# Retention outputs in two visits of TensorE instead of three, and the last product of the kernel in two halves

## The chip, the cores and the metric

The kernel runs on one core of a Trainium2 chip. A core has a matrix engine (TensorE, PE in the profile, its weight loads PEld), a vector engine (VectorE, DVE), a scalar engine (ScalarE, ACT), GpSimd (POOL) and SyncE (SP), which here issues the transfers. Each takes its instructions in its own order and waits on semaphores for the others. Operands lie in SBUF, and TensorE writes to PSUM, which has eight banks of 2 KB for each of 128 partitions. The metric is the device time of one execution in microseconds (us).

## The reference

Two parts follow each other. The first is a retention layer over 4 sequences of 768 tokens with 8 heads of 64:

```python
for t in range(S):
    state = gamma * state + einsum('bhd,bhe->bhde', k[:, :, t], v[:, :, t])
    y[:, :, t] = scale * einsum('bhd,bhde->bhe', q[:, :, t], state)
```

Its output, as 3072 tokens of 512 features, goes through a two-layer block: `h = x @ w_in` (512 to 2048), `g = where(h > 0, h, exp(min(h, 0)) - 1)`, `out = g @ w_out` (2048 to 512). All is fp32.

## The kernel before

**Blocks.** The 3072 tokens are taken in six blocks of 512, each of four chunks of 128 tokens; the code counts blocks (`tb`) from 0, the text from one, so block six is `tb` 5. A sequence has six chunks, so that blocks two and five (`tb` 1 and 4) hold the end of one sequence and the start of the next, and there the powers of gamma start again in the middle of the block.

**Large products.** Nearly all of TensorE's time goes to the two layers. They use the seven-product scheme for 2x2 blocks of matrices, once or twice nested, with sums of inputs and outputs on VectorE (`quarters_of`, the L945 and L815 groups; L990 and L1407 for outputs) and copies of partial results on ScalarE (L986, L1297, L1403). Their results go to PSUM banks that the code calls pa (two buffers), pb and pd (one each). A fp32 product instruction appears as two records in the trace.

**Retention.** Time runs through it in half chunks of 64 tokens. A block takes three kinds of 64x64 products, each of which uses one quarter of the array: a half of its rows (`sub` or `a`) and a half of its columns (`c`).

- scores (L331): q against k in each half chunk, 128 records for a block; VectorE masks them (L342).
- states (L371): k against v in each half chunk, 128 or 112 records; VectorE adds the states up, one after the other (L383), the last of a block into `carry`.
- outputs: within a half chunk, v against the masked scores (`within`, L427, 128 records for a block), and across, the state against q (`across`, L442, 128 or, where a sequence starts, 112 records). Both add up in the same PSUM tile y. VectorE then multiplies y by powers of gamma into the input x of the first layer (L417, tiles xt or xb).

A product that takes array rows of half `a` must not write to a bank to which one of the other half still writes. Within products of half chunk `sub` use row half `sub`; across products of head half `a` use row half `a`. In the kernel before, a bank y[sub] belongs to one half chunk and holds all heads, so across products with `a` equal to `sub` can follow the within products at once, and the others (`other` = 1) need a wait. The wait goes through VectorE: it copies eight numbers a partition out of each bank (`seen`, L411), and the other products wait for that copy.

**The visits.** A block's outputs are made in halves of two chunks (`outputs(tb, pp)`), two banks each, from the pool `ps_r` of four buffers (tag "r"), which scores, states and outputs use in turn. `outputs_step` runs the generators. In blocks two to four (`tb` up to 3) step 0 does half 0 up to the copies; step 1 ends half 0 (other products, two multiplications) and begins half 1; step 2 ends half 1. In blocks five and six step 0 begins half 0, step 1 begins half 1, step 2 ends both. So TensorE leaves the large products for outputs three times a block.

The order on each engine is the order of the Python calls. The steps stand between large products by hand: in the loop over `inner` for block two, in the first `sec` loop for block three, in the loop over `ORDER1` for block four, and at the places `VISITS` of the last loop for blocks five and six.

**The end.** `inner_end` makes the last seven products. The last one (k = 3) adds into the bank pa that already holds three products; VectorE then adds the kept part `k[:, 0, 1]`, and a store of 128 KB ends the kernel (L1465 to L1467).

Of the kernel before, what the change touches and what calls it, by code (L numbers as in the profile page):

```python
# [28 lines left out]
def kernel(  # L29
# [281 lines left out]
    def state(tb, n):  # L311

        if n % (2 * CPB) == 0:
            return carry[(tb + n // (2 * CPB)) % 2]
        if (tb, n) == (0, 3):

            return xt[0].rearrange("p a t -> p (a t)")[:, 0:256].rearrange("p (h e) -> p h e", e=D)

        k = raw[tb * CPB + (n - 1) // 2][1][:, 1].rearrange("p h d -> p (h d)")
        return k[:, (n - 1) % 2 * 256 : ((n - 1) % 2 + 1) * 256].rearrange("p (h e) -> p h e", e=D)  # L320

    def fresh(tb, n):

        return (tb * 2 * CPB + n) % (S // D) == 0
# [122 lines left out]
    def outputs_of_first():  # L447

        y = [bank(x).rearrange("p a (b x d) -> p (a b) x d", b=2, x=2) for x in "bd"]
        for x in range(2):  # L450
# [19 lines left out]
            if not x:  # L470
                yield

    def outputs_step(tb, step):

        if step == 0:
            held["y"] = [outputs(tb, pp) for pp in range(2)]
        early_end = tb <= 3
        if step and early_end:
            next(held["y"][step - 1], None)
        elif step == 2:  # L480
            for g in held["y"]:
                next(g, None)
        if step < 2:
            next(held["y"][step])
            next(held["y"][step])

    half = [slice(0, TH), slice(TH, TB)]

# [368 lines left out]
    def done(name):  # L857
        slot, lasts = where.pop(name), lasting.pop(name)
        if lasts or wanted and wanted[0][0][0] == 1:
            slots.append((slot, lasts))  # L860
        fetch()
# [518 lines left out]
    def second_big(nb, behind_last):  # L1380
        ts, kept2 = {}, {}
        ends = nb == NB - 1

        def input_parts(j):
            x = INPUT2[j]
            t = (slots_e, slots_s)[len(ts) % 2]
            b11, b12, b21, b22 = (quarter(x, a, b) for a in range(2) for b in range(2))
            yield from quarters_of(t, b11, b12, b21, b22, nc.gpsimd if j == 1 else nc.vector)
            ts[j] = {1: b11, 2: b21, 3: b22, 4: t[3], 5: t[0], 6: t[1], 7: t[2]}

        def product(j, k, ps, begin):
            name = (nb + 2, j, k)
            w = where[name].rearrange("p (f d) -> p f d", f=4)
            for f in range(4):
                nc.tensor.matmul(  # L1395
                    ps, lhsT=w[:, f, :], rhs=ts[j][k][:, f // 2, f % 2, :], start=(begin and f == 0), stop=(f == 3),
                    skip_group_check=True,
                )
            done(name)

        def copy(ps):
            m = small.tile([P, TH], FP32, name="ms", tag="ms")
            nc.scalar.copy(m, ps)  # L1403
            return m

        def add(o, x, y):
            nc.vector.tensor_tensor(out=o, in0=x, in1=y, op=ALU.add)  # L1407

        part = lambda x: bank(x)[:, 0]

        def inner(j):
            res = (two if j in (6, 7) else mpool).tile([P, 2, 2, TH], FP32, name="res", tag="m")
            pa = part("a")
            product(j, 1, pa, True)
            m1 = copy(pa)
            pb = part("b")
            product(j, 2, pb, True)
            add(res[:, 0, 0], pb, m1)
            yield
            product(j, 6, pa, False)  # L1420
            u2 = copy(pa)
            pd = part("d")
            product(j, 7, pd, True)
            yield
            product(j, 5, pa, False)
            add(res[:, 1, 1], pd, copy(pa))
            yield
            product(j, 3, pa, False)
            nc.scalar.copy(res[:, 0, 1], pa)  # L1429
            yield  # L1430
            product(j, 4, pd, False)
            add(res[:, 1, 0], pd, u2)
            sum_up(j, res.rearrange("p d t c -> p (d t c)"))

        def inner_end(j):

            res = mpool.tile([P, 2, 2, TH], FP32, name="res", tag="m")
            to = out_of[nb][1, 0].rearrange("p (d t c) -> p d t c", d=2, t=2)
            k = kept2[6].rearrange("p (d t c) -> p d t c", d=2, t=2)
            pa = part("a")  # L1440
            product(j, 1, pa, True)
            m1 = copy(pa)
            pb = part("b")
            product(j, 2, pb, True)
            add(res[:, 0, 0], pb, m1)
            yield
            product(j, 6, pa, False)
            u2 = copy(pa)
            pd = part("d")
            product(j, 7, pd, True)  # L1450
            m7 = copy(pd)
            yield
            add(u2, u2, k[:, 1, 0])
            add(u2, pd, u2)
            product(j, 5, pa, False)
            add(res[:, 1, 1], pa, m7)
            yield
            add(res[:, 0, 0], res[:, 0, 0], k[:, 0, 0])
            nc.sync.dma_start(to[:, 0, 0], res[:, 0, 0])
            add(res[:, 1, 1], res[:, 1, 1], k[:, 1, 1])  # L1460
            pb = part("b")
            product(j, 4, pb, True)
            add(res[:, 1, 0], pb, u2)
            nc.sync.dma_start(to[:, 1], res[:, 1])
            product(j, 3, pa, False)  # L1465
            add(res[:, 0, 1], pa, k[:, 0, 1])
            nc.sync.dma_start(to[:, 0, 1], res[:, 0, 1])  # L1467

        def store(name, h):
            nc.sync.dma_start(out_of[nb][int(name[1]) - 1, int(name[2]) - 1], h)  # L1470

        def sum_up(j, m):

            kept2[j] = m
            if j == 2:
                add(m, kept2[1], m)
                store("C11", m)
            elif j == 6:
                add(m, kept2[1], m)
            elif j == 5:  # L1480
                add(m, kept2[6], m)
                add(kept2[6], kept2[6], kept2[7])
                add(kept2[7], m, kept2[7])
# [12 lines left out]
        for at, j in enumerate(BIG2):  # L1496
            cur = (inner_end if j == 4 and ends else inner)(j)
            next(cur)
            if j == 1:
                yield "tail"  # L1500
            for _ in before:
                pass
            if at:
                yield "first"
            some(changes, {2: 1, 3: 4, 7: 1, 5: 2}.get(j, 0))
            parts = input_parts(BIG2[at + 1]) if at + 1 < 7 else iter(())
            if j == 1:

                next(cur)
                yield "elu"  # L1510
                some(parts, 2)
            else:
                some(parts, 2)
                if at == 6:
                    behind_last()
                next(cur)
                yield "middle"
            next(cur)
            if j != 1:
# [179 lines left out]
    def retention_step(tb, step):  # L1699
        if step == 0:  # L1700
            scores(tb, 0)
            scores(tb, 1)
        elif step == 1:
            states(tb, 0)
            states(tb, 1)
        else:
            outputs_step(tb, step - 2)
# [123 lines left out]
    for nb in range(NB):  # L1831
# [83 lines left out]
        for at, (j, sub) in enumerate(ORDER1):  # L1915
# [18 lines left out]
            if nb == 0:  # L1934
                if at == 0:
                    scores(3, 1)
                elif at == 1:
                    retention_step(3, 3)
            if at == 7:
                run(tail)  # L1940
                seeds(0, 1, first=True)
# [2 lines left out]
            if nb == 0:  # L1944
                if at == 0:
                    states(3, 1)
                elif at == 1:
                    retention_step(3, 4)
                    run(tail)
            side(at, 2)  # L1950
# [81 lines left out]
        if more:  # L2032
# [1 line left out]
                scale_v(groups[0] * CPB + n)  # L2034
        step = 0
        VISITS = [
            (0, "end"), (1, "end"), (2, "middle"), (2, "end"), (3, "middle"),
            (5, "first"), (5, "end"), (6, "first"), (6, "middle"), (6, "end"),
        ]
        LOADS = [(3, "middle"), (3, "end"), (4, "first"), (4, "middle")]  # L2040
# [70 lines left out]
```

## Time and profile before

| what | value |
|---|---|
| median of 3 runs | 608.09 us (608.03 to 612.51) |
| the profiled execution's own time | 607.38 us |
| its span, first to last instruction | 605.6 us |
| TensorE busy | 599.0 us, 99% |
| VectorE busy | 508.6 us, 84% |
| ScalarE, GpSimd busy | 261.5 us and 98.3 us |
| granted TensorE clock | 1.000 |

The page gives busy times by engine, the chain of waits that ended last, and groups of equal instructions. A timeline row has start, length, engine, line, operation, output and inputs with shape, and the count of records merged; square brackets hold the idle time before it and what ended that. A merged row's length runs from its first start to its last end, and a record's end overlaps the next one's start. The chain of waits gives start, length and piece, with a product's length up to the next one's start.

### The profile page before, as it was taken

How to read it: one execution, taken by the hardware profiler on the slowest of the kernel's cores; microseconds unless marked ns; L12 is line 12 of the kernel's file. 1: busy time of each engine (PE TensorE's matmuls, PEld its weight loads, DVE VectorE, ACT ScalarE, POOL GpSimd, SP SyncE). 2: the span in 40 equal slices, each digit the busy share in tenths (PEclk: the TensorE clock that was granted, in tenths of full speed). 3: DMA queues.
4: the chain of work that ended last, by engine and by line, in shares of the span. 5: the costliest groups of instructions: out<-in, count | busy, mean ns of one | idle time of the engine just before them, and what ended most of it. 6: DMA issues, size and time to landing. Idle time of an engine off the chain costs nothing.

```text
span 605.6 us, 13752 instructions
## 1 busy us (share of the span) xinstructions
PE 599.0 (99%) x5510; PEld 491.9 (81%) x5510; DVE 508.6 (84%) x779; ACT 261.5 (43%) x448; POOL 98.3 (16%) x77
## 2 busy tenths in 40 slices
PE   7999999999999999999999999999999999999997
PEld 5865568888889999888766888888888866888886
DVE  6778889989899886899898887898658999779785
ACT  6898734205543112247589210100236779611110
POOL 2020000000230110000797000120000398000000
PEclk9999999999999999999999999999999999999999
DMA  8797578789968998698976445874555676556552
GB/s 324 274 407 289 189 232 254 227 244 268 351 224 264 354 348 294 204 307 272 352 248 217 129 131 153 273 277 112 197 167 151 172 221 194 160 150 188 154 152 115
DMA packets 85680, 139.85 MB, mean 231 GB/s; under 512 B 6896, under 2 KB 46576, under 8 KB 80880
## 3 DMA queue, kind: packets, MB, share of 16 engines
q1 hardware_dynamic: 85616, 138.96, 70.9%
q8 instruction: 44, 0.72, 0.5%
q14 instruction: 20, 0.16, 0.1%
HBM read 105.12 MB, written 33.82 MB: 229 GB/s over the span
## 4 chain that ended last, share of the span: by engine, by line
PE 97%; DMA 1%; DVE 1%; issue 0%; SPq 0%; ACT 0%
PE pa L1395 16%; PE pa L1286 9%; PE pd L1395 8%; PE pa L784 5%; PE pd L1286 5%; PE x L1349 4%; PE pb L1395 4%; PE pa L978 4%; PE pa L557 3%; PE x L647 3%; PE pb L1286 2%; PE pd L784 2%; PE pa L647 2%; PE pa L1336 2%; PE sc L331 2%; PE kv L371 2%
## 5 line engine op out<-in xcount | busy, mean ns | idle before, releaser
L1403 ACT COPY ms<-pa 128x256 f32<-128x256 f32 x41 | 15.3, 372 | 106.5 <-PE pa L1395 103.5
L1395 PE MATMUL pa<-gC,wq 128*128 128x256 f32 x240 | 56.8, 381 | 0.0
L1395 PEld LDWEIGHTS pa<-gC,wq 128*128 128x128 f32 x240 | 45.1, 190 | 7.3 <-issue 1.0
L305 POOL TENSOR_TENSOR chunk<-chunk,vf 128x512 f32<-128x512 f32 x15 | 19.6, 1316 | 153.6 <-DMA chunk<-in_qkv_dram 104.7
L1362 ACT ACTIVATE r<-r 128x512 f32<-128x512 f32 x64 | 40.4, 631 | 2.0
L1407 DVE TENSOR_TENSOR res<-pd,ms 128x256 f32<-128x256 f32 x26 | 11.0, 422 | 28.2 <-PE pd L1395 17.5
L1297 ACT COPY m<-pa 128x512 f32<-128x512 f32 x32 | 18.7, 584 | 35.0 <-PE pa L1286 31.8
L1395 PE MATMUL pd<-w_all,wq 128*128 128x256 f32 x120 | 28.3, 379 | 0.0
L1363 DVE SCALAR_TENSOR_TENSOR gC<-r,gC 128x512 f32<-128x512 f32 x24 | 27.9, 1169 | 0.0
L926 POOL TENSOR_TENSOR wp<-wp 128x512 fp32r<-128x512 f32 x6 | 8.8, 1467 | 116.5 <-DMA scratch_dram<-wi 102.2
L183 ACT ACTIVATE w_all<-wraw 128x1024 uint32<-128x1024 uint32 (+1 forms) x19 | 19.2, 1009 | 15.1 <-PE x L647 9.6
L1395 PEld LDWEIGHTS pd<-w_all,wq 128*128 128x128 f32 x120 | 22.8, 190 | 3.1
L1857 POOL TENSOR_TENSOR chunk<-chunk,w_all 128x512 f32<-128x512 f32 x4 | 5.1, 1287 | 124.4 <-ACT w_all L1297 124.4
L1377 DVE TENSOR_TENSOR gC<-w_all,gC 128x1024 f32<-128x1024 f32 x20 | 24.2, 1260 | 0.0
L1349 PE MATMUL x<-xl,wq 128*128 128x512 f32 x64 | 23.7, 457 | 0.0
L1395 PE MATMUL pa<-w_all,wq 128*128 128x256 f32 x96 | 22.9, 381 | 0.0
L1395 PE MATMUL pa<-ts,wq 128*128 128x256 f32 x96 | 22.9, 381 | 0.0
L185 ACT ACTIVATE w_all<-wraw 128x1024 fp8e4<-128x1024 f32 (+1 forms) x19 | 22.6, 1190 | 0.6
L1395 PE MATMUL pd<-ts,wq 128*128 128x256 f32 x96 | 22.7, 379 | 0.0
L557 PE MATMUL pa<-xb,w_all 128*128 128x512 f32 x48 | 21.5, 597 | 0.0
L1429 ACT COPY res<-pa 128x256 f32<-128x256 f32 x13 | 4.8, 373 | 38.1 <-PE pa L1395 38.1
L213 DVE CUSTOM_DVE_ANT_0 w_all<-wraw,w_all 128x2048 uint16<-128x2048 uint16 (+1 forms) x19 | 20.1, 1059 | 0.8
(369 smaller groups left out, 1598.6 us busy)
## 6 DMA issues: line engine op xcount, KB each, us to landing
wq<-scratch_dram SPq DMA_DIRECT2D x231, 256.0 KB, 3.4
chunk<-in_qkv_dram SPq DMA_DIRECT2D x22, 1024.0 KB, 7.5
wraw<-in_w_dram SPq DMA_DIRECT2D x15, 1024.0 KB, 5.9
scratch_dram<-wp SPq DMA_DIRECT2D x8, 512.0 KB, 3.9
out_dram<-res SPq DMA_DIRECT2D x7, 512.0 KB, 3.4
scratch_dram<-gT SPq DMA_DIRECT2D x12, 256.0 KB, 3.6
wq<-scratch_dram SPq DMA_DIRECT2D x24, 128.0 KB, 2.9
scratch_dram<-w_all SPq DMA_DIRECT2D x12, 256.0 KB, 3.1
```

The costliest lines, as they stand in the source:

```text
L185: nc.scalar.activation(top, hi.bitcast(FP32), AF.Copy, scale=2.0**-120, saturate=False)
L213: vec.tensor_tensor(out=flat, in0=c, in1=flat, op=ALU.add)
L557: nc.tensor.matmul(hp, lhsT=w[n][:, fi, j // 2, j % 2, :], rhs=xb[:, j, :], start=(j == 0), stop=(j == 3))
L647: nc.tensor.matmul(X[j][:, d, :], lhsT=w[j][:, d * P : d * P + P], rhs=x[j], start=(n == 0 and d == 0), stop=at_end, skip_group_check=True,)
L784: nc.tensor.matmul(ps[:, fi, :], lhsT=w[:, fi, j2, :], rhs=x[:, j2, :], start=(begin and fi == 0 and j2 == 0), stop=(j2 == 1), skip_group_ ...
L978: nc.tensor.matmul(ps, lhsT=w[:, f, :], rhs=ts[j][k][:, f, :], start=(begin and f == 0), stop=(f == 3), skip_group_check=True,)
L1286: nc.tensor.matmul(ps[:, f, :], lhsT=w[:, f, :], rhs=big_xs[j][k], start=(begin and f == 0), stop=True, skip_group_check=True,)
L1349: nc.tensor.matmul(joined(ps), lhsT=where[name][:, c : c + P].bitcast(F32R), rhs=x[:, k], start=(not third and c == 0), stop=(k == 1), ski ...
L1362: nc.scalar.activation(r, r, AF.Exp, scale=-1.0)
L1363: return lambda: nc.vector.scalar_tensor_tensor(g, r, -1.0, h, ALU.add, ALU.max)
L1377: nc.vector.tensor_tensor(out=quarter(to, r, t), in0=quarter(x, r, t), in1=quarter(y, r, t), op=op)
L1395: nc.tensor.matmul(ps, lhsT=w[:, f, :], rhs=ts[j][k][:, f // 2, f % 2, :], start=(begin and f == 0), stop=(f == 3), skip_group_check=True,)
```

## The change

Blocks two to six get a new function, `outputs_of_block`, which handles the whole block with four banks, y[sub][a], one for each half chunk and head half. All within products come first, in one visit; only the banks with `sub` unequal to `a` are copied from (`seen`, two instead of four a block). All across products follow in the next visit, in order of chunks. The multiplications come by head half: the first half behind the across products, the second half in the third step, which has no products any more. Where a block wraps round a sequence, each multiplication is cut in two (256 columns instead of 512). Block one keeps the old functions.

Two steps move: block four's second step goes behind the next product, and in block five the second step goes from (2, "end") to (3, "first").

In `inner_end` the kept part is added right after product 5, and product 3 is made in two halves of 128 columns in banks of their own, each with its own addition and its own store of 64 KB.

```diff
+    def outputs_of_block(tb):
+        y = [[ps_r.tile([P, 2, 4, D], FP32, name="y", tag="r") for _ in range(2)] for _ in range(2)]
+        ms = [raw[tb * CPB + n] for n in range(CPB)]
+        for n in range(CPB):
+            for u in range(2):
+                for a in range(2):
+                    pt = ms[n // 2 * 2 + a][0][:, 1].rearrange("p h c -> p (h c)")
+                    for c in range(2):
+                        for sub in range(2):
+                            nc.tensor.matmul(
+                                y[sub][a][rows(c), u, n, :], lhsT=ms[n][1][rows(sub), 0, head(a, u, c), :],
+                                rhs=pt[rows(sub), (n % 2 * HP + 2 * u + c) * D :][:, 0:D],
+                                start=(n == 0 and u == 0), stop=False, skip_group_check=True,
+                            )
+        for sub in range(2):
+            seen = epool.tile([P, 8], FP32, name="seen", tag="seen")
+            nc.vector.tensor_copy(seen.rearrange("p (u n) -> p u n", u=2), y[sub][1 - sub][:, :, :, 0])
+        yield
+        for n in range(CPB):
+            for other in range(2):
+                for u in range(2):
+                    for a in range(2):
+                        sub = a ^ other
+                        if fresh(tb, 2 * n + sub):
+                            continue
+                        for c in range(2):
+                            p = 2 * u + c
+                            nc.tensor.matmul(
+                                y[sub][a][rows(c), u, n, :], lhsT=state(tb, 2 * n + sub)[rows(a), p, :],
+                                rhs=ms[n][0][rows(a), 0, p, rows(sub)], start=False, stop=True, skip_group_check=True,
+                            )
+        at = [chunks[tb * CPB + n][1] for n in range(CPB)]
+        runs = [slice(0, CPB)] if at[2] == at[0] + 2 else [slice(0, 2), slice(2, CPB)]
+        for a in range(2):
+            for sub in range(2):
+                for r in runs:
+                    i = at[r.start]
+                    nc.vector.tensor_tensor(
+                        out=of_sub(x_of(tb)[:, 2 * a : 2 * a + 2, r.start * C : r.stop * C], sub), in0=y[sub][a][:, :, r],
+                        in1=of_sub(etab[:, a, :, i * C : (i + r.stop - r.start) * C], sub), op=ALU.mult,
+                    )
+            if not a:
+                yield
...
         if step == 0:
-            held["y"] = [outputs(tb, pp) for pp in range(2)]
-        early_end = tb <= 3
-        if step and early_end:
-            next(held["y"][step - 1], None)
-        elif step == 2:
-            for g in held["y"]:
-                next(g, None)
-        if step < 2:
-            next(held["y"][step])
-            next(held["y"][step])
+            held["y"] = outputs_of_block(tb)
+        next(held["y"], None)
...
-        def product(j, k, ps, begin):
+        def product(j, k, ps, begin, columns=slice(0, TH), last=True):
...
             add(res[:, 1, 1], pa, m7)
+            add(res[:, 0, 1], pa, k[:, 0, 1])
...
-            product(j, 3, pa, False)
-            add(res[:, 0, 1], pa, k[:, 0, 1])
-            nc.sync.dma_start(to[:, 0, 1], res[:, 0, 1])
+            for x, c in (("a", slice(0, P)), ("d", slice(P, TH))):
+                ps = part(x)[:, 0:P]
+                product(j, 3, ps, True, c, x == "d")
+                add(res[:, 0, 1, c], ps, res[:, 0, 1, c])
+                nc.sync.dma_start(to[:, 0, 1, c], res[:, 0, 1, c])
...
-                elif at == 1:
-                    retention_step(3, 3)
...
                 elif at == 1:
+                    retention_step(3, 3)
                     retention_step(3, 4)
...
-            (0, "end"), (1, "end"), (2, "middle"), (2, "end"), (3, "middle"),
+            (0, "end"), (1, "end"), (2, "middle"), (3, "first"), (3, "middle"),
```

More of the change, by code (lines that the diff above doesn't have):

```diff
@@ L473, in outputs_step @@
+    of_sub = lambda t, sub: t.rearrange("p u (n s c) -> p u n s c", s=2, c=D)[:, :, :, sub]
     def outputs_step(tb, step):
         if step == 0:
[L476 to L485 removed]
+            held["y"] = outputs_of_block(tb)
+        next(held["y"], None)
@@ L1395, in product @@
                 nc.tensor.matmul(
-                    ps, lhsT=w[:, f, :], rhs=ts[j][k][:, f // 2, f % 2, :], start=(begin and f == 0), stop=(f == 3),
+                    ps, lhsT=w[:, f, :], rhs=ts[j][k][:, f // 2, f % 2, columns], start=(begin and f == 0), stop=(f == 3),
                     skip_group_check=True,
                 )
-            done(name)
+            if last:
+                done(name)
         def copy(ps):
```

## The prediction

> **What bounds the kernel.** I read the page's top first, then the chain of waits, then the timelines of TensorE and VectorE around each visit that the change touches.
>
> ```profile
> span 605.6 us, 13752 instructions
> PE 599.0 (99%) x5510; PEld 491.9 (81%) x5510; DVE 508.6 (84%) x779; ACT 261.5 (43%) x448; POOL 98.3 (16%) x77
> PE 97%; DMA 1%; DVE 1%; issue 0%; SPq 0%; ACT 0%
> ```
>
> TensorE is busy for 99% of the span and is 97% of the chain that ends last. So a microsecond taken from TensorE's own queue is a microsecond of the result, unless another engine then fails to keep up; VectorE, at 84%, is the only one near. The next question is what one visit to the 64x64 attention products costs, beyond its products. From the chain of waits (start, length, piece):
>
> ```profile
> 401.11 1.73 PE pd L1395 x8
> 402.84 2.02 PE sc L331 x128
> 404.86 1.92 PE pa L1395 x8
> 406.79 1.73 PE pd L1395 x8
> 408.51 1.73 PE pa L1395 x8
> 410.24 2.01 PE kv L371 x112
> 412.25 1.92 PE pa L1395 x8
> 414.18 1.73 PE pb L1395 x8
> ```
>
> An undisturbed product of 8 records takes 1.727 us; the one behind each visit takes 1.92. One visit with all it disturbs: 401.11 to 406.79 is 5.68 us, less two products (3.45), so 2.22 us for 128 records, and likewise 2.21 for 112 (408.51 to 414.18, rounded). Now TensorE's timeline in block six, where the outputs come in three visits:
>
> ```profile
> 417.46 1.89 PE L1395 MATMUL pd<-ts,wq 128*128 128x256 f32 x8
> 419.29 1.16 PE L427 MATMUL y<-chunk 64*64 64x64 f32 x64
> ...
> 420.84 1.99 PE L1395 MATMUL pa<-gC,wq 128*128 128x256 f32 x8
> ...
> 424.49 1.16 PE L427 MATMUL y<-chunk 64*64 64x64 f32 x64
> ...
> 426.05 1.99 PE L1395 MATMUL pa<-gC,wq 128*128 128x256 f32 x8
> ...
> 430.04 1.89 PE L1395 MATMUL pa<-gC,wq 128*128 128x256 f32 x8
> ```
>
> From 417.46 to 430.04 is 12.58 us. In it stand 36 records of large products (8, 8, 8, 8 and 4), at 1.727/8 each 7.77 us; 4.81 are left for three visits with 96, 96 and 64 records. The same subtraction gives 4.78 to 4.82 in blocks two to five. Records cost the same in every visit: 256 in three visits take 4.81, 128 in one take 2.22, so three visits and two differ by 4.81 - 2 x 2.22 = 0.37, one visit's fixed price.
>
> **The change part by part.** *Two visits for three, blocks two to six.* The products are the same ones (128 records within the chunks, 112 or 128 across). Each block loses one fixed price: 4.80 becomes 4.44, or 4.43 with 112 records. 5 x 0.36 = 1.8 us on TensorE's own path. That the new nesting keeps 14.6 ns per record (0.466 us per 32) I take from the scores: L331 runs row halves innermost and column halves next, the order that the new first visit has, and it is one of the 2.22 us rows.
>
> *Four banks at once.* The first visit now needs all four banks of the pool, the last two of which hold the states of the block's second half. Their last reader, the additions at L383, ends at 67.0 in block two (visit at 68.8), 360.6 in block five (365.2) and 417.0 in block six (419.3): free in time. In block four it starts at 245.25 and takes 0.42, to 245.67, and the visit starts at 245.62, with the fourth bank needed from its fifth instruction. Bounds: 0, and 0.15 if the weight load must wait too; I take 0.1.
>
> *VectorE.* Two small copies (0.156 us each) go per block: -0.31. Blocks three, four and six keep four multiplications of 512 columns (0.68). Blocks two and five, whose chunks wrap round a sequence, have eight of 256 instead; the row of that width is L383's 0.423 us: 8 x 0.42 - 4 x 0.68 = +0.64, with the copies +0.33. The Trainium skill, "VectorE: DVE Perf Modes", section on the TRN2 errata, speaks against this edit: each instruction pays a fixed cost, so tiles should have 512 elements or more. By its formula, an estimate, the eight cost 0.63 more than the four; by rows back to back (starts at 425.66, 426.00 and 426.33 for 256 columns, 0.60 apart for 512) only 8 x 0.34 - 4 x 0.60 = 0.32; the sum is the same by either, for the work is beside TensorE. It is hidden: in block two VectorE idles 1.99 us before 80.41, in block five 1.29 before 381.53.
>
> *The added wait.* The first multiplications waited for the first half's products; now they wait for the whole second visit, and VectorE's queue stands behind them. Block three is the dense place:
>
> ```profile
> 196.82 1.27 DVE L417 TENSOR_TENSOR xt<-y,etab 128x512 f32<-128x512 f32 x2
> 198.02 0.22 DVE L411 COPY seen<-y 128x8 f32<-128x8 f32 x2
> ...
> 200.35 0.29 DVE L990 TENSOR_TENSOR res<-pd,ms 128x128 f32<-128x128 f32 x1 [0.18 <-ACT ms L986]
> ...
> 204.44 0.29 DVE L990 TENSOR_TENSOR res<-pd,ms 128x128 f32<-128x128 f32 x1 [0.61 <-PE pd L978]
> ```
>
> The new second visit ends at 197.53 (188.72 + 2.12 + 4.56 of products + 2.12), its last result 0.15 later, so 196.82 becomes 197.68: 0.86 late. Behind stand the input sums L815 and L945 and then the L990 addition of 204.44, which frees bank pd for the product at 205.13. Of the 0.86, 0.22 goes with the copies and 0.18 with the idle time at 200.35; 0.46 is left, against 0.61 of idle time, of which TensorE, now 0.36 earlier, takes all but 0.25. The addition then ends 0.2 later relative to TensorE, and the product had 0.29 to spare: about 0.1 us remains. Cost 0, and up to 0.46 if I misplace the visit's end. In block four the addition that frees bank pd ends about 257.5, and the bank is wanted at 258.8; in block five VectorE is at 383.4 where ScalarE lets it go on at 383.9; in block six the copies end at 424.95 and are needed from about 425.2. All are covered, the last by 0.2.
>
> *The queues.* Block four's second step moves behind one more product, block five's behind four more; the steps issue products and VectorE work alone, no transfers. SyncE, GpSimd and ScalarE keep their order. Chunk loads of blocks five and six follow the across products, which come earlier or within 0.5 us of before: no cost.
>
> *The last product.* Four instructions of 256 columns (1.727) become eight of 128; L978's row of that form is 0.893 per 8 records, so 1.787: +0.06. They start in fresh banks, without the 0.05 for which the last product now waits on VectorE. The sum with the kept part moves ahead (0.34 on VectorE, beside a product of 1.73). After the last record the addition is 0.29 (L990, 128 columns) for 0.43: -0.14. The last store is 64 KB for 128; stores here land in 2.0 us (256 KB) and 1.7 (128 KB), so between 0 and -0.15 more; I take -0.1. Sum -0.23, bounds -0.3 and 0.
>
> **Sum.** -1.8 + 0.1 - 0.23 = -1.9 us. The profiled execution took 607.38 (span 605.6 and 1.8 around it): 605.5. The median shown, 608.09, is 0.7 above that execution, so 606.2 for the median.
>
> **The rivals.** *VectorE takes it back (slower than before).* The place is block three and its likes, the mechanism the added wait: if nothing covered the 0.86 in any of the five blocks, 5 x 0.86 = 4.3 us come on, 608.09 - 1.9 + 4.3 = 610.5. It decides from the point where the first multiplication is more than about 1 us later than before, since 0.1 is left. For it: 84% busy, 0.1 us of room in block three. Against: idle times after every visit, and 0.2 to 0.5 us of room elsewhere. The Trainium skill, "TensorEngine Tiling (Array Packing)", section PSUM Bottleneck, warns of just this: array tiling speeds TensorE and not the emptying of the banks, which should be done in wide accesses. Chance 0.12.
>
> *The price isn't per visit.* If 0.36 belonged to the switch between the two kinds of products, which stays, only the end's 0.23 comes: 607.9. Against: visits of a single kind (scores, states) show the full price, and inside a visit the switch takes 0.04. Chance 0.12.
>
> *The order of the records costs.* If two banks in turn broke the overlap of the four quarters of the array, the first visits would take twice as long: 5 x 128 x 14.6 ns = +9.3, so 615.5. Against: L331 does the same. Chance 0.03.
>
> **How the numbers follow.** The forecast has 0.70; 0.03 is left for a gain I don't see. The range 605.0 to 608.3 holds the forecast with its bounds (end 0.1 better, the bank 0.05 worse, block three 0.5 worse), the level of the median, which moves by some 0.7 between executions, and the second rival: together 0.82. One per cent, 6 us, is about what a measurement of this kernel tells from no change. All but the third rival and a tail of the first lie within: faster 0.01, same 0.95, slower 0.04.
>
> **What would show it.** Right: two visits of 2.22 us per block, the product behind each the only longer one; TensorE's busy time near 597; the last store issued 0.15 us earlier after the last record. Wrong: idle time of the weight loads before L978 in block three or before the first visit of block four; a visit's length other than 2.0 us for 128 records; multiplications of 256 columns well over 0.42.

## The result and the profile after

The changed kernel takes 607.39 us (median of 22 runs, 605.80 to 609.81), the kernel before 609.51 in its 22 runs beside them (607.74 to 613.10). The ratio is 0.9967, 95% interval 0.9954 to 0.9980: 2.0 us less, 1.2 to 2.8 by the interval. The forecast was 606.2, 1.9 us less; the change was met to 0.1 us, and the 1.2 us between 606.2 and 607.39 are the level of the kernel before, 1.4 us higher in these runs than in the three shown.

The first profiled execution of the changed kernel was one of its longest: its own time is 609.81. From its page:

```profile
span 608.0 us, 13773 instructions
PE 599.4 (99%) x5518; PEld 493.1 (81%) x5518; DVE 508.6 (84%) x779; ACT 261.7 (43%) x448; POOL 98.9 (16%) x77
PEclk9999999999999999899999999999999999999999
```

TensorE has 8 records more (the last product in halves) and is not busy for less time. The 8 in the row of the granted clock points at most of what makes this execution long. Between 240 and 249 us the weight loads of a visit waited 2.07 us for its chunk, and the clock then fell to 0.67 for 5 us; together they put the large products 3.3 us behind those of the third profile used below. The table by windows shows the clock (columns: window, length, busy time and instruction count of each engine, granted clock, DMA share, GB/s):

```profile
238.00:244.00 6.00, 4.07 (x78) 3.15 (x76) 1.09 (x2) 2.29 (x4) 0.51 (x1) 0.99 0.87 279
244.00:249.00 5.00, 5.00 (x86) 3.86 (x80) 2.95 (x6) 0.05 (x1) 0.53 (x1) 0.67 0.80 257
```

These are scores and states, ahead of the block's outputs, and the two later profiles of this kernel have a clock of 1.000. So I read the change from the same work in both traces. TensorE's timeline in block six after the change, which answers to the rows shown of before:

```profile
420.57 1.89 PE L1434 MATMUL pd<-ts,wq 128*128 128x256 f32 x8
422.39 2.09 PE L483 MATMUL y<-chunk 64*64 64x64 f32 x128
424.41 2.00 PE L1434 MATMUL pa<-gC,wq 128*128 128x256 f32 x8
...
430.09 1.99 PE L1434 MATMUL pa<-gC,wq 128*128 128x256 f32 x8
431.92 1.03 PE L1325 MATMUL pa<-xt,wq 128*128 128x256 f32 x4
432.78 1.89 PE L1434 MATMUL pa<-gC,wq 128*128 128x256 f32 x8
```

The same 36 records of large products and the same 256 records of outputs took from 417.46 to 430.04 before, 12.58 us, and now from 420.57 to 432.78, 12.21: 0.37 less, with one visit less. The product that followed the third visit (431.92) is now one of the ordinary length, 1.03 where it had 1.13. VectorE in block three, the dense place of the prediction:

```profile
197.91 1.29 DVE L511 TENSOR_TENSOR xt<-y,etab 128x512 f32<-128x512 f32 x2
...
204.73 0.28 DVE L1029 TENSOR_TENSOR res<-pd,ms 128x128 f32<-128x128 f32 x1
```

The multiplications start at 197.91, after the whole second visit. The addition at 204.73 had 0.61 us of idle time ahead of it before; it has none now, and TensorE's weight loads have no wait between 200 and 210 us.

Executions of one kernel lie up to 5.4 us apart in these runs, and a single pair of profiles can mislead. For the account below I use a third profile of the changed kernel (span 605.2, clock 1.000), which has neither the fallen clock nor the long wait, against the shown profile of before (span 605.6). The large products come in the same order in both, so the difference of their starts tells where time went:

| place | predicted, us | in the traces, us |
|---|---|---|
| start-up (first transfers) | 0 | +1.09 |
| outputs, block two | -0.37 | -0.52 |
| outputs, block three | -0.36 | -0.35 |
| a wait at 227 us | 0 | +0.39 |
| a wait for a chunk at 241 us | 0 | +0.23 |
| outputs, block four, with the wait for the bank | -0.26 | -0.49 |
| a wait at 258 us | 0 | +0.42 |
| outputs, block five | -0.37 | -0.52 |
| outputs, block six | -0.36 | -0.36 |
| the end | -0.23 | -0.30 |

The sum is -0.4, the difference of the spans. Start-up, 227 and 241 us belong to the execution: a second profile of the kernel before has the 0.39 at 227 as well (its weight loads wait 0.7 us there, as in the changed kernel) and a wait for the chunk at 241 (0.17), which is 0.70 in a further profile with the old outputs (end only, below), and start-up differs by up to 0.9 us among the three profiles of the changed kernel (block two's scores start at 57.66, 58.34 and 58.59). What belongs to the change is -2.22 for the outputs, +0.42 at 258 us and -0.30 at the end: -2.1, against 2.0 measured. Two things in it need an explanation that the prediction does not have: blocks two, four and five gained more than a visit's price, and at 258 us something was given back.

### The profile page after: what moved, and what is told of

It is laid out like the page before. It is cut to its first block, busy times and chain, and to the rows that moved or that the text cites. A ratio compares the mean times of both kernels' runs of the same rounds, so it can differ in the third digit from the quotient of the medians.

```text
span 608.0 us, 13773 instructions
## 1 busy us (share of the span) xinstructions
PE 599.4 (99%) x5518; PEld 493.1 (81%) x5518; DVE 508.6 (84%) x779; ACT 261.7 (43%) x448; POOL 98.9 (16%) x77
## 4 chain that ended last, share of the span: by engine, by line
PE 74%; DMA 2%; DVE 1%; issue 0%; SPq 0%; ACT 0%; DVEq 0%
PE pa L1434 16%; PE pa L1325 9%; PE pd L1434 8%; PE pa L823 5%; PE pd L1325 4%; PE x L1388 4%; PE pb L1434 4%; PE pa L1017 3%; PE pd L823 2%; PE pa L1375 2%; PE pb L1325 2%; PE pa L1388 2%; DMA chunk<-in_qkv_dram 1%; PE kv L371 1%; PE pd L1017 1%; PE y L483 1%
## 5 line engine op out<-in xcount | busy, mean ns | idle before, releaser
L1434 PE MATMUL pa<-gC,wq 128*128 128x256 f32 (+1 forms) x240 | 55.6, 378 | 0.0
```

Source lines behind the costliest of these rows:

```text
L1434: nc.tensor.matmul(ps, lhsT=w[:, f, :], rhs=ts[j][k][:, f // 2, f % 2, columns], start=(begin and f == 0), stop=(f == 3), skip_group_check ...
```

## The experiments

**Undoing the two parts.** One kernel has the new outputs with the old end, one the old outputs with the new end. Three visits keeps the new function, its four banks and its one long first visit, and cuts the second visit in two after two chunks:

```diff
         for n in range(CPB):
+            if n == 2:
+                yield
             for other in range(2):
...
                     )
-            if not a:
-                yield
```

> The changed kernel once more. Theory (one fixed price of 0.36 us per visit saved in five blocks, 0.16 more in the three blocks whose across products skip a half chunk, 0.2 at the end, less what VectorE gives back): 2.0 us below the kernel before, ratio 0.9967. In the profile, the idle times of TensorE at 132, 150 and 227 us (0.25, 0.16 and 0.66 us in the first profile) come again if the change causes them; if they came from one late store (VectorE waited 1.04 us for a store of tile m at 93 us), they go, and TensorE's visits keep their lengths of 2.12, and 1.95 with 112 records.

In the profile of this run the idle times at 132 and 150 us are gone, and the one at 227 is there; the second profile of the kernel before has all three. So the change does not cause them.

> The changed kernel with the old end. Theory: 1.8 us faster than before (0.997), most of the whole; the rival that the end brings the gain, and the rival that the price is not per visit: within 0.3 us of before (0.9995 or more).

> The kernel before with the new end alone (last product in two halves, kept part added ahead). Theory: 0.2 us faster than before (0.9996), TensorE's 128-record price unchanged; the rival that the end brings the gain: 2 us faster (0.997). The last store is issued about 0.3 us after the last record starts to end, 0.15 sooner than before, and everything ahead of 600 us is as before.

> The changed kernel with its four banks kept, but the across products in two visits again (two chunks each), so that each block has three visits; the multiplications come behind the last one. Theory (the price is per visit): five visits of 0.36 us come back, 1.8 us slower than the changed kernel, about 0.3 to 0.7 faster than before (0.999). Rival (four banks and the split by head bring the gain, not the number of visits): as the changed kernel, 2 us faster than before (0.9967).

| kernel | median, us | ratio to before, 95% interval |
|---|---|---|
| before | 610.09 | |
| changed, again | 608.84 | 0.9966 (0.9947 to 0.9986) |
| outputs only | 607.96 | 0.9963 (0.9942 to 0.9984) |
| end only | 610.75 | 0.9999 (0.9976 to 1.0022) |
| three visits | 610.16 | 0.9994 (0.9967 to 1.0022) |

These are 12 runs of each, and 35 of the kernel before. The gain is that of the outputs. With four banks, the same order of records and one visit more it is no longer seen, though by the times alone the step from 0.9966 to 0.9994 is not clear, since the two intervals overlap; the trace settles it, as shown below. The end alone cannot be measured; its 0.3 us in the trace are 0.0005 of the time. TensorE's timeline of three visits in block six:

```profile
420.08 1.89 PE L1434 MATMUL pd<-ts,wq 128*128 128x256 f32 x8
...
430.60 1.16 PE L503 MATMUL y<-chunk 64*64 64x64 f32 x64
431.69 1.13 PE L1325 MATMUL pa<-xt,wq 128*128 128x256 f32 x4
432.66 1.89 PE L1434 MATMUL pa<-gC,wq 128*128 128x256 f32 x8
```

From 420.08 to 432.66 is 12.58 us, the same as before to the hundredth. In blocks two and five, however, this kernel is 0.2 us ahead of the kernel before with the same number of visits; more on that below.

**More visits.** If a visit has a price of its own, visits can be added where nothing else happens. In the last loop of the second layer, which has no retention, eight products of no use are put in 17 times:

```diff
+            if not more and step >= 1 and s != BIG2[-1]:
+                extra = [any_bank() for _ in range(2)]
+                for e in range(8):
+                    r, c = e % 2, e // 2 % 2
+                    nc.tensor.matmul(
+                        extra[r][rows(c), 0, 0:D], lhsT=cmask[rows(r), :], rhs=cmask[rows(r), :], ...
```

> The changed kernel with 17 visits more: in the last loop of the second layer, where all operands lie ready and nothing is kept back, eight 64x64 products of no use are put between products of 128x128, 17 times over. The theory (a visit has a fixed price of 0.36 us beside its records): a visit costs 0.36 us and its 16 records of 14.6 ns, 0.23 us, together 0.59 us; 17 of them make the kernel 10.1 us longer than the changed kernel. The rival (there is no price by the visit, only by the record): 17 x 0.23 = 4.0 us. A third case, in which the stretch is not bound by TensorE and takes them up: under 2 us.

Measured: 617.22 us in four runs, ratio 1.0111 (1.0069 to 1.0153). Against the changed kernel's 0.9967 that is 0.0144, or 8.8 us (5.4 to 12.1 by the ends of the two intervals), which 10.1 fits and 4.0 does not. The trace is sharper. TensorE's timeline:

```profile
530.19 1.89 PE L1434 MATMUL pd<-w_all,wq 128*128 128x256 f32 x8
532.01 0.46 PE L2099 MATMUL x<-cmask 64*64 64x64 f32 x16
532.40 1.99 PE L1434 MATMUL pa<-ts,wq 128*128 128x256 f32 x8
534.23 1.89 PE L1434 MATMUL pd<-ts,wq 128*128 128x256 f32 x8
```

From 530.19 to 534.23 are 4.04 us for two products of 1.727 and a visit: 0.59 us. Less 16 records of 14.6 ns, 0.36 are left. All 17 visits cost the same to 1 ns by the records' starts: 0.485 up to the next product, and 0.104 more in that product. A wait for operands or banks, or a lack of anything on another engine, does not come out so even. The price is the visit's.

**VectorE's room in block three.** The prediction's second number of weight was that 0.1 us of room is left there. Two multiplications that nobody uses are put ahead of the block's first ones:

```diff
+        for _ in range(2 if tb == 2 else 0):
+            more_work = epool.tile([P, 512], FP32, name="r", tag="r", bufs=3)
+            nc.vector.tensor_tensor(out=more_work, in0=etab[:, 0, 0, 0:512], in1=etab[:, 0, 1, 0:512], op=ALU.mult)
```

> The changed kernel with two multiplications of 512 columns more on VectorE, ahead of block three's first multiplication (about 1.2 us of VectorE's time, by the 1.29 us that two such take in the trace). The theory (the first multiplications of block three now wait for the whole second visit, and the last sum before the projection's product is ready only 0.17 us ahead of it): TensorE stands still for 0.9 to 1.1 us ahead of the product that reads block three's result, and the kernel is up to 1.1 us longer than the changed kernel. The rival (VectorE has room of a microsecond or more there): TensorE does not wait, and the time is that of the changed kernel.

Measured: 608.38 us, ratio 0.9978 (0.9952 to 1.0005); the difference of 0.7 us from the changed kernel lies within the intervals. The trace has it. VectorE's timeline:

```profile
198.01 1.29 DVE L509 TENSOR_TENSOR r<-etab 128x512 f32<-128x512 f32 x2
199.22 1.29 DVE L514 TENSOR_TENSOR xt<-y,etab 128x512 f32<-128x512 f32 x2
...
205.74 0.28 DVE L1032 TENSOR_TENSOR res<-pd,ms 128x128 f32<-128x128 f32 x1
```

And the weight loads of TensorE:

```profile
204.52 0.97 PEld L1020 LDWEIGHTS pa<-ts,wq 128*128 128x128 f32 x8
206.08 0.97 PEld L1020 LDWEIGHTS pd<-ts,wq 128*128 128x128 f32 x8 [0.59 <-DVE res L1032]
```

TensorE now waits for exactly the addition that the prediction named. Against TensorE's products, block three's first multiplications came 1.08 late, for 0.12 of the 1.2 us put in filled an idle time; another 0.3 went in idle time behind them (0.19 of it a wait for ScalarE), so that the last addition came 0.78 late, and the weight loads of the product, with all that follows, 0.67. The room was 0.11 us. My expectation of 0.9 to 1.1 had left out these idle times.

**Why 112 records took 1.94 and not 2.10.** A sequence that starts in a block saves one half chunk's across products, 16 records. In the states (L371, 112 records) this saves nothing: 2.10 us for 2.12 with all 128. In the new second visit it saved 0.17. My first idea was the order:

```diff
-        for n in range(CPB):
-            for other in range(2):
+        for other in range(2):
+            for n in range(CPB):
```

> The changed kernel with the two loops of the second visit exchanged, so that the records of one row half are all written before those of the other. In the trace of the changed kernel the second visit of blocks two, four and five (112 records, where one half chunk is left out) took 1.94 us and not the 2.10 that 112 records by the first visit's rate and price would take. The theory (the two records left next to each other by what is left out lie in different row halves and overlap): with the loops exchanged the visit takes 2.10 us, 0.16 us more in each of the three blocks, 0.5 us in all; visits of 128 records are no shorter. The rivals: the order within a visit decides nothing, and it stays at 1.94; or records of one row half after each other do not overlap at all, and every second visit becomes longer, by up to the 2.2 us that it took again.

Measured: 609.15 us, ratio 0.9979 (0.9952 to 1.0007), and in the trace the visits of blocks two, four and five take 1.944, 1.934 and 1.946 us, counted from the end of the product ahead to the start of the one behind. In the third profile of the changed kernel they take 1.94, 1.90 and 1.95. The theory falls, in that it does not matter whether the two remainders are neighbours; the one visit that became longer did so by 0.04 us, far from the 2.2 of the second rival, so that falls too. What is left is that both row halves lose records within one visit, nearly in whatever order. That can be put to the test by leaving out 16 records in either manner:

```diff
                         if fresh(tb, 2 * n + sub):
                             continue
+                        if tb == 2 and n == 1 and sub == 0 or tb == 5 and n == 1 and a == 0:
+                            continue
```

> The changed kernel with work left out, for a look at lengths alone: in the second visit of block three the 16 records of one half chunk (eight in either row half), in that of block six 16 records that all lie in one row half. Both visits have 128 records and take 2.12 us in the changed kernel. The theory (the two row halves work side by side, and a visit lasts as long as the fuller of them): block three's visit takes 1.90 to 1.95 us, block six's stays within 0.02 of 2.12. The rival (the length goes by the number of records): both take 1.89, 16 x 14.6 ns less. A second rival (what counts is that the left-out records belong to one half chunk): block six's is the shorter by some other amount, and not by row halves.

TensorE's timeline of that kernel, block three and block six (first records of the visit, and the product behind it):

```profile
196.26 0.27 PE L503 MATMUL y<-chunk,carry 64*64 64x64 f32 x2
...
198.12 1.16 PE L1019 MATMUL pa<-ts,wq 128*128 128x128 f32 x8
...
425.55 0.27 PE L503 MATMUL y<-chunk,carry 64*64 64x64 f32 x2
...
427.58 1.99 PE L1436 MATMUL pa<-gC,wq 128*128 128x256 f32 x8
```

Both visits have 112 records. Block three's, with eight left out in either row half, is over after 1.86 us; block six's, with 16 left out in one row half, after 2.03, exactly as long as the 2.03 that 128 records take (in the third profile of the changed kernel, 425.21 to 427.24). These lengths run from a visit's first record; the expectations count from the end of the product ahead, 0.09 earlier, which makes them 1.95 and 2.12, as the theory has it. A visit lasts as long as its fuller row half. That holds to some 0.05 us: block four's second visit, whose left-out records would come first, takes 1.81 where those of blocks two and five take 1.85. The kernel before has signs of it too: its visits of 88 (245.62 to 247.18) and 96 records (68.80 to 70.36) both take 1.56 us, those of 120 (73.99 to 76.02) and 128 (195.04 to 197.07) both 2.03. This is the term that the prediction lacked: the kernel before had the left-out records of the two row halves in two different visits (one of 120 and one of 24 records in block two), where neither saves; the new second visit has them together. It explains that three visits is 0.2 us ahead of before in blocks two and five, whose cut by chunks keeps the two together as well, and in block six, where nothing is left out, is not.

**What is given back at 258 us.** The timeline of the kernel before, all engines, cut to the rows that matter:

```profile
249.87 1.03 PE L1286 MATMUL pd<-tq,wq 128*128 128x256 f32 x4
...
250.95 0.90 SPq L679 DMA_DIRECT2D scratch_dram<-wp  x2
...
255.49 1.03 PE L1286 MATMUL pa<-xt,wq 128*128 128x256 f32 x4
...
256.56 0.59 ACT L1297 COPY gC<-pa 128x512 f32<-128x512 f32 x1 [4.98 <-DVE gC L1301]
...
257.04 0.63 ACT L924 ACTIVATE wp<-w_all 128x512 fp32r<-128x512 f32 x1
...
258.20 0.73 PEld L1286 LDWEIGHTS pa<-w_all,wq 128*128 128x128 f32 x4 [0.36 <-ACT m L1297]
```

And of the changed kernel, third profile:

```profile
251.26 1.03 PE L1325 MATMUL pd<-tq,wq 128*128 128x256 f32 x4
...
252.34 0.90 SPq L718 DMA_DIRECT2D scratch_dram<-wp  x2
...
255.85 1.03 PE L1325 MATMUL pa<-xt,wq 128*128 128x256 f32 x4
...
256.91 0.58 ACT L1336 COPY gC<-pa 128x512 f32<-128x512 f32 x1 [3.95 <-PE pa L1325]
...
257.82 0.63 ACT L963 ACTIVATE wp<-w_all 128x512 fp32r<-128x512 f32 x1 [0.32 <-DMA scratch_dram<-wp]
...
258.97 0.51 PEld L1325 LDWEIGHTS pa<-w_all,wq 128*128 128x128 f32 x3 [0.77 <-ACT m L1336]
```

ScalarE may write wp again once a store of it has left. In both kernels that store is issued 1.08 us after the start of the product pd<-tq,wq, and ScalarE's copy, behind which it comes to wp, starts 1.07 and 1.06 us after the start of the product pa<-xt,wq. So both go with TensorE, and what has changed is TensorE's way from one product to the other: 5.62 us before, 4.59 now, 1.03 less. Before, two visits stood between them (120 and 32 records), now one of 112; the visit's price, the records that moved ahead into the first visit and the half chunk left out in one visit make up the difference. The bracket of 256.56 names VectorE, whose addition ended at that very moment, but VectorE did not hold the copy back: it starts as long after the product as in the kernels where VectorE was done long before.

ScalarE therefore came to wp 6.09 us after the issue before, when the store was out, and would now come after 5.06, as it does in the executions without a wait. In the third profile it goes on after 5.48 us, the copy behind, which TensorE needs, is late by 0.42, and TensorE's weight loads wait 0.77 us where they waited 0.36. Neither of the two profiles of the kernel before has a wait at this store, nor those of end only and three visits. Of ten profiles with the new outputs in two visits seven have it (0.21 to 0.64 us); in these the store had landed 5.3 to 5.7 us after its issue, in the three others (the first profile, extra visits and the first profile of scores and states put together, below) after 4.1 to 4.3. With the old outputs it took 5.3 to 5.6, so the transfers are not slower than before; it is the room that is less. That the wait costs, and from where it comes, is read from the traces; a version with a second buffer for wp was not tried.

**Executions that are some 3 us longer.** In the profiles of the changed kernel again and of outputs only, 88.8 and 88.6 us pass from block four's second visit of outputs to block five's scores, in that of extra visits 85.6; between 296 and 328 us the first two lose 2.6 us. Whether the change brings that was the question of two more profiles:

> The kernel before, unchanged, profiled a second time. The question is whether the 2.9 us that some executions lose between 252 and 341 us (a wait of ScalarE for a store, then of TensorE for VectorE) are a matter of the execution or of the change. If of the execution, the kernel before may show them too, and the changed kernel not always; if of the change, the kernel before does not show them here either, and the changed kernel does. One look on each side can only lean one way.

> The changed kernel, unchanged, profiled a third time, beside the second profile of the kernel before. If the change brings the loss between 252 and 341 us, the stretch from block four's second output visit to block five's scores takes 88.5 us as in two of the profiles so far; if it is a matter of the execution, 85.6 us as in two others, or either.

The third profile of the changed kernel has 86.0 us from block four's second visit to block five's scores (253.08 to 339.06), of which 0.4 is the wait at 258, and nothing of the loss. The second profile of the kernel before, which has no wait at 258, loses 2.6 us between 296 and 328 against its first. The first row of it, from the weight loads of the kernel before:

```profile
298.32 0.30 PEld L1349 LDWEIGHTS x<-xr,wq 128*128 128x128 f32 x2 [0.61 <-DMA wq<-scratch_dram]
```

and the like of the changed kernel's second profile:

```profile
297.33 0.30 PEld L1388 LDWEIGHTS x<-xr,wq 128*128 128x128 f32 x2 [1.06 <-DMA wq<-scratch_dram]
...
321.35 0.30 PEld L1388 LDWEIGHTS x<-xl,wq 128*128 128x128 f32 x2 [1.20 <-DVE x L957]
```

Both begin with a late weight transfer, and then TensorE waits for VectorE several times, though VectorE was in time in the undisturbed executions. The loss is one of the execution, and both kernels have it in some: it stands in four of the 14 profiles, one of three with the old outputs and three of ten with the new ones in two visits. Why that transfer is late in some executions stays open.

**One step further.** If a visit costs 0.36 us, block four's scores and states, which come in four visits of 64 records, could come in two:

```diff
-        if at == (3, "first"):
+        if at == (4, "first"):
             scores(3, 0)
-        elif at == (4, "first"):
             states(3, 0)
...
                 if at == 0:
                     scores(3, 1)
+                    states(3, 1)
...
-                if at == 0:
-                    states(3, 1)
-                elif at == 1:
+                if at == 1:
                     retention_step(3, 3)
```

> The changed kernel with the scores and the states of block four put together: its four visits for these become two, the number of records stays. The theory (0.36 us by the visit): TensorE is through with the first layer 0.7 us sooner than in the changed kernel, and the time would be 0.9955 of the kernel before. The rival (what TensorE gains there is given back in waits for VectorE and for the transfers of the gate between 258 and 328 us): the time is that of the changed kernel, 0.9967 of the kernel before, or up to 0.5 us longer, if the states come later than VectorE wants them.

> The kernel with block four's scores and states put together, profiled a second time, since in the first profile the granted clock fell within both of its visits. The theory (0.36 us by the visit): the two visits of 128 records take 2.12 us each, where the four of 64 take 1.19 each, and with the products behind them TensorE is 0.72 us ahead of the changed kernel after both. The rival: the larger visits make VectorE late, and TensorE waits for a bank after them, by up to the 0.72.

Measured: 608.95 us, ratio 0.9970 (0.9939 to 1.0001), no different from the changed kernel. In the first profile the granted clock is down to 0.72 from 218 to 224 us, in the first merged visit and behind it; the second visit waited for a chunk, at full clock, and not for the clock as the expectation above says. In the second profile the span is 604.2 us beside 605.2 of the changed kernel on the same chip, of which 0.38 is start-up. TensorE's timeline:

```profile
216.69 1.16 PE L331 MATMUL sc<-chunk 64*64 64x64 f32 x64
217.67 1.11 PE L371 MATMUL kv<-chunk 64*64 64x64 f32 x64
218.71 1.16 PE L1017 MATMUL pa<-ts,wq 128*128 128x128 f32 x8
```

One visit of 2.02 us stands where two stood of 1.10 and 1.09 (210.81 to 211.91, and 218.35 to 219.44): 0.17 less. With the gap of 0.09 ahead of a visit and the 0.10 in the product behind it, the large products come 0.36 us earlier for each visit saved, as the theory has it. At 258 us ScalarE then waits 0.64 us for the store in place of 0.32, and TensorE gives back 0.32; that is the store's own length in this execution, for ScalarE comes to it 5.06 us after the issue, as before, and in the first profile there is no wait. So 0.6 us is left in the trace, 0.19 of it from waits for a chunk and for the bank that are shorter than in the other profile; the time cannot tell that from nothing.

## Why the prediction was right, and where it was not

- **One visit's fixed price, 0.36 us:** right, and the heart of it. Blocks three and six gained 0.35 and 0.36; 17 added visits cost 0.36 each beside their records; a third visit put back brings block six to the 12.58 us of before. Of the price, 0.104 lies in the product behind the visit. The rival that the price is not per visit falls. The Trainium skill, "TensorEngine Tiling (Array Packing)", section Key Properties, says that a change of the tiling mode drains TensorE, without a price. The trace fits that: ahead of each of the 17 added visits the weight loads stand idle for 0.33 us, and nothing is named that they wait for. The 0.36 us is what going to the small products and back costs here; that a drain is what it goes to is not shown.
- **The records' order:** right. From the end of the product ahead to the start of the one behind, the new first visits take 2.118 us for 128 records in blocks five and six, and the scores' visits the same 2.118.
- **"4.43 with 112 records":** the term that was mis-sized. It came from a states visit of 112 records, where all 16 left-out records lie in one row half. In the outputs they lie in both, and the pair of visits takes 4.27: 0.16 us more gain in each of blocks two and five, and 0.2 in block four, where the half chunk left out comes first. I had priced records where I should have priced the fuller row half.
- **Four banks at once, +0.1 in block four:** right. The visit there took 2.19 us instead of 2.12, 0.08 more; the carry addition that it needs ended at 246.51 in the third profile, 0.05 after the visit's first record.
- **VectorE:** right in kind. The multiplications of 256 columns run at 0.33 us each, the bound by rows and not the 0.42 of a lone one: block two's first four took 1.42 us. The Trainium skill, "VectorE: DVE Perf Modes", section on the TRN2 errata, has a fixed cost for each instruction; the trace shows a smaller one for instructions back to back (0.33 us apart for 256 columns and 0.60 for 512), and no wait of TensorE goes back to it.
- **The added wait:** right, with its terms on the high side. Against the large products of before, block three's first multiplications came 0.58 us late where 0.86 was worked out, since they start 0.13 ahead of the product behind the visit and not 0.15 after its start. The addition that frees pd came 0.14 late against TensorE, where 0.2 was expected, and was covered, with 0.11 us of room by the added load, about 0.1 by the prediction. The rival that VectorE takes it all back did not come, though it is 0.11 us away in this block: 0.78 us more cost 0.67.
- **"SyncE, GpSimd and ScalarE keep their order ... no cost":** the step that failed. ScalarE keeps its order, but between the issue of a store and the copy after which ScalarE needs its buffer TensorE now has 1.03 us less to do, and the store takes no less time than before in most executions. The room at that store was 6.09 - 5.48 = 0.61 us in the third profile, ScalarE came 1.03 earlier, and TensorE lost 0.42. I had looked at what the change makes late and not at what it makes early.
- **The end, -0.23:** the traces have -0.30, at the end of its bounds; it is too small to be measured.
- **TensorE's busy time near 597:** wrong as a sign. It was 599.4 and 598.3. In the shown profile of before all but 0.1 of TensorE's 6.6 us of idle time lie in the first 30 and the last 11 us of the span, so its busy time goes with the span, slow start and fallen clock included, and shows nothing of single visits.
- **"One per cent, 6 us, is about what a measurement of this kernel tells":** too coarse. With 22 executions of each kernel the interval is 0.8 us to either side.

The two errors, about -0.5 and +0.42, nearly cancel, which is why the sum is better than its terms. That it came within 0.1 us is to this extent luck: in three of the ten profiles the second error is not there at all.

## What to carry to other kernels

Where TensorE alternates between large products and small ones that use a quarter of the array, count the visits before the records: here one costs as much as 24 records, and it can be measured by itself with a few useless visits in a quiet loop. Price such a visit by its fuller row half, and group work so that what is left out empties both halves in the same visit. When a step moves, ask not only who comes late, but which engine comes early, because work ahead of it went away, and which transfer it then finds unfinished; and take a second profile of both kernels before a microsecond of difference is explained.

## What was not expected of the hardware

- Records in different row halves do not hold each other up over a whole visit: 112 records took 1.86 us with both halves relieved and 2.03 with one, and the order of the loops counted for 0.04 at most.
- A useless visit of 16 records costs 0.59 us to within 1 ns, 17 times in a row.
- The granted clock fell in two of the 14 profiled executions, to 0.67 for 5 us and to 0.72 for 6 us, both times among block four's scores and states; the other twelve have a mean of 1.000 or 0.999.
- Executions of one and the same kernel lay up to 7 us apart (608.02 to 615.07 in 35 of the kernel before); in the profiles this is start-up (up to 0.9 us among three of the changed kernel), a late chunk (up to 2.1 us of wait), one late weight transfer with the waits behind it (2.6 us) and the clock.
